# A retention mixer in three stages: batches in order at the start, and a weight conversion with three VectorE steps

## The chip, the cores and the metric

The kernel runs on one core of a Trainium2 chip. Times are device microseconds (us) of one execution, from start to end on that core. The inputs lie in the chip's memory at the start, and the output must lie there at the end.

## The reference

Three layers follow each other. The first is retention over 8 batches of 576 rows with 8 heads of 64, the second a token mixer of low rank followed by a two-layer network with 512, 2048 and 512 columns, the third a channel mixer on each row and the row before it. Cut to what is computed:

```
# q, k, v: (8, 8, 576, 64) float32
scores = matmul(q, k.T) / sqrt(64)
ret    = scores * D           # D[h, i, j] = gamma[h] ** (i - j) for i >= j, else 0
x      = matmul(ret, v)       # float32, then (8, 576, 512)

h  = x.T @ U @ V              # U: (576, 32), V: (32, 576), float64
u  = x + h.T
x  = u + maximum(u @ w_ch1, 0) @ w_ch2     # (512, 2048) and (2048, 512), float64

xk = mu_k * x + (1 - mu_k) * x_prev        # x_prev: one row earlier, zero in row 0
xr = mu_r * x + (1 - mu_r) * x_prev
k  = maximum(xk @ w_k, 0)                  # (512, 1024), float64
v  = k * k @ w_v                           # (1024, 512), float64
out = sigmoid(xr @ w_r) * v                # (512, 512), float64
```

U, V and the five weight matrices arrive as float64, and the kernel makes float32 of them on the chip.

## The kernel before

The rows of all batches are 4608, in nine blocks of 512. Every dense product is computed in three passes on pairs of tiles, a rounded high part (names ending in `h`) and the rest (names ending in `l`): high by high, low weight by high, high weight by low.

*Stage one* covers retention, the token mixer and the first dense product. A batch is cut into nine chunks of 64 rows. In a chunk TensorE computes the scores (`scores`, line 358), the product of the queries with the state carried over from the earlier chunks (`inter`, line 383), the chunk's addition to the state (`own`, line 399) and its own output (line 411). VectorE multiplies the scores by the decay table (tile `pm`, line 370), scales the product with the state (`y`, line 432), adds to the state (`w`, line 444; in the first chunk a copy, line 442) and adds up the output, transposed, in `xt` (line 450; in the first chunk a copy, line 448). The scores and the decay of a chunk are issued one step ahead. After every second chunk four transposes bring 128 rows into their natural order (`natural`, line 458) and four small products add to x.T @ U (`low_rank`, line 479). Once a batch has all nine chunks, `low_rank_sum` collects this, eight small products and additions (`mix`, lines 508 and 512) make u in `xt`, and `mix_store` splits it into high and low parts (lines 191 and 192), stores it (lines 519 and 520) and puts sixteen dense tiles on the list `ready`. A dense tile (`hidden`, tile `h`) is twelve matmuls at line 204, then ReLU on ScalarE (line 210) and a store (line 211). From here on they fill TensorE between the chunks.

*Weights.* `convert` makes float32 of a 128x512 piece of float64, in stages that `slot` moves on by one: the load (line 157); `flush`, an absolute value on ScalarE (line 100); `fill`, four VectorE steps (lines 106, 107, 111 and 116) that take the high words, set what is too small to zero, shift and mask the exponent and put sign and fraction together; and `split`, where ScalarE rounds to the high part (line 124) and GpSimd subtracts (line 125). U comes first, then group 0 of w_ch1 (`w1_0`, four pieces), V (two pieces of 288 columns), and groups 1 to 3.

*What sets the order.* Up to line 744 the code's own order is the order on each engine (`manual_schedule`), and each engine works through its own list and waits where something isn't there. Transfers are issued by SyncE, in order as well. The list `seq` in lines 587 to 592 gives the chunks: four chunks of batch 0, then one of batch 1 and one of batch 0 in turn until batch 0 ends, then the rest of batch 1, then the other batches one after another. `step_of` issues one step of it: loads of q, k and v ahead (line 652), the chunk, a slot of conversion (line 671), mixes if no dense tile is ready, and up to two dense tiles (lines 675 and 678) with what is due between them (transposes, `low_rank`, mixes). With one mix after each of its three passes, a dense tile also takes mixes along, and moves the conversions on by one where there are none (line 550). In lines 522 and 523 the dense tiles that are ready when batch 1 ends are sorted, so that those of the first group of w_ch1 come first.

*Stage two* is the second dense product (`project`, lines 237, 238 and 241), for which the stored h is loaded again and split, with the conversions of w_ch2 (line 696) and of the third layer's weights w_k, w_r and w_v beside it. *Stage three* is the channel mixer: `key_chunk` (products at line 760, square at line 766), `gate_tile` (line 779) and `value_tile` (line 794). From line 746 on the framework's scheduler sets the order.

Of the kernel before, what the change touches and what calls it, by code (L numbers as in the profile page):

```python
# [9 lines left out]
F32 = mybir.dt.float32  # L10
F32R = mybir.dt.float32r
BF16 = mybir.dt.bfloat16
U32 = mybir.dt.uint32
# [26 lines left out]
def retention_mixer_kernel(ctx: ExitStack, tc: tile.TileContext, io):  # L40
# [43 lines left out]

    TINY = float(np.array(897 << 20, np.uint32).view(np.float32))


    def convert(fetch, parts, p, n, after=None, eng=nc.gpsimd):  # L90
        got = {}

        def load():
            got["raw"] = fetch()

        def flush():
            w = got["raw"].bitcast(U32).rearrange("p (n t) -> p n t", t=2)
            got["lo"], got["hi"] = w[:, :, 0], w[:, :, 1]
            got["a"] = cv.tile([128, 512], F32, tag="ca", name="ca", bufs=2)[:p, :n]
            nc.scalar.activation(got["a"], got["hi"].bitcast(F32), AF.Abs)  # L100

        def fill():
            h, l = parts()
            a, lo, hi = got["a"], got["lo"], got["hi"]
            f = got["f"] = cv.tile([128, 512], F32, tag="cf", name="cf", bufs=3)[:p, :n]
            nc.vector.scalar_tensor_tensor(f, a, TINY, hi.bitcast(F32), op0=ALU.is_ge, op1=ALU.mult)  # L106
            nc.vector.tensor_scalar(  # L107
                a.bitcast(U32), f.bitcast(U32), 3, 0x3FFFFFFF,
                op0=ALU.logical_shift_left, op1=ALU.bitwise_and,
            )  # L110
            nc.vector.scalar_tensor_tensor(  # L111
                f.bitcast(U32), f.bitcast(U32), 0xC0000000, a.bitcast(U32),
                op0=ALU.bitwise_and, op1=ALU.bitwise_or,
            )
            whole = f if l is not None else h
            nc.vector.scalar_tensor_tensor(  # L116
                whole.bitcast(U32), lo, 29, f.bitcast(U32),
                op0=ALU.logical_shift_right, op1=ALU.bitwise_or,
            )

        def split():
            h, l = parts()
            if l is not None:
                nc.scalar.copy(h, got["f"])
                eng.tensor_tensor(l, got["f"], h.bitcast(F32), op=ALU.subtract)

        return [load, flush, fill, split] + ([after] if after else [])

    waiting, going = [], []

# [168 lines left out]
    with ExitStack() as st:  # L299
# [120 lines left out]
        def by_pair(x):  # L420
            return x.rearrange("p (a r) i -> p a r i", r=2)

        def leave(i):
# [14 lines left out]
            if c < NL - 1:  # L438
                d = t[:, :, 128:256].rearrange("p r (a x) -> p a r x", x=D)
                new = a2.tile([128, NP, D], F32, tag="wst", name=f"w{b}_{c}", bufs=4)  # L440
                if c == 0:
                    nc.vector.tensor_copy(by_pair(new), d)
                else:
                    nc.vector.tensor_tensor(by_pair(new), d, by_pair(wst[b]), op=ALU.add)
                wst[b] = new
            own_x = t[:, :, 0:128].rearrange("p r (a i) -> p a r i", i=L)
            if c == 0:
                nc.vector.tensor_copy(x, own_x)
            else:
                nc.vector.tensor_tensor(x, own_x, by_pair(y), op=ALU.add)  # L450

# [62 lines left out]
        def mix_store(b):  # L514
            o = (b + 1) * BT - b * S
            u = xt.pop(b)
            split_u(b, BT - o, u[:, :, :o], o)
            split_u(b + 1, 0, u[:, :, o:], S - o)
            nc.sync.dma_start(u_blk[b][:, :, BT - o:], u[:, :, :o])
            nc.sync.dma_start(u_blk[b + 1][:, :, :S - o], u[:, :, o:])  # L520
            ready.extend((b, f) for f in range(NF))
            if b == 1:
                ready.sort(key=lambda x: (x[1] >= 4, x))
            if b == B - 1:
                ready.extend((b + 1, f) for f in range(NF))

# [55 lines left out]
                    lambda s=s: nc.scalar.copy(vst[64:96, s], low[64:96].bitcast(F32)), nc.vector,  # L582
                ))

        LEAD = 4
        seq = [(0, c) for c in range(LEAD)]
        for c in range(NL - LEAD):
            seq += [(1, c), (0, c + LEAD)]  # L590
        seq += [(1, c) for c in range(NL - LEAD, NL)]
        seq += [(b, c) for b in range(2, B) for c in range(NL)]
        N = len(seq)
        FIRST = 2 * NL
        units = []
        for i, (b, c) in enumerate(seq):
            if c % 2 == 0:
# [50 lines left out]

        def step_of(i):
            b, c = seq[i]  # L650
            first = i < FIRST
            load_to(i + (7 if first else 4))
            if i + 1 < N:
                nb, ncx = seq[i + 1]
                if ncx % 2 == 0:
                    scale_k(nb, ncx // 2)
            if i + 1 < N:
                scores(i + 1)
            inter(i)
            if i + 1 < N:  # L660
# [1 line left out]
            own(i)  # L662
            leave(i)
            if c % 2 == 1 or c == NL - 1:
                wait = 4 if i < 8 else 2
                plan(i + 1, natural, b, c // 2)
                plan(i + wait, low_rank, b, c // 2)
                if c == NL - 1:
                    plan(i + wait, low_rank_sum, b)
                    plan(i + wait + 1, later, b)  # L670
            if first and (i < 10 or i % 2 == 0):
                slot()
            if not ready:
                mixes(4)
            hidden(1)
            for fn, args in due.pop(i, []):
                fn(*args)
            hidden(1)

        for i in range(N):  # L680
            step_of(i)
# [203 lines left out]
```

## Time and profile before

| | us |
|---|---|
| median of 3 runs | 1497.29 (1496.33 to 1497.86) |
| the profiled execution | 1495.31 |
| its span, first to last instruction | 1493.40 |
| TensorE busy | 1443.6 (97% of the span) |
| TensorE weight loads, beside its matmuls | 1164.9 (78%) |
| VectorE busy | 611.7 (41%) |
| ScalarE busy | 491.2 (33%) |
| GpSimd busy | 239.0 (16%) |
| granted TensorE clock, mean | 0.98 of full speed |

The span is what the trace covers; the execution's own time is 1.91 us longer. A share of busy time is a mean over the stages, and the rows further down take the span apart. In the views, PE is TensorE, PEld its weight loads, DVE VectorE, ACT ScalarE, POOL GpSimd and SPq the issue of transfers by SyncE. A granted clock (PEclk) of 1.00 is 2.4 GHz and 0.50 is 1.2 GHz; what lies between is a mean over a stretch. A releaser is what ended a wait.

### The profile page before, as it was taken

The page shows a single profiled execution, that of the slowest core. Times are in us where ns is not written, and L with a number is a line of the kernel's source. Part 1 is how long each engine was busy: PE and PEld are TensorE (multiplying, and loading weights), DVE is VectorE, ACT ScalarE, POOL GpSimd, SP SyncE. Part 2 cuts the span into 40 slices and gives each one's busy share as a digit, 9 for nine tenths or more (in the row PEclk, how much of TensorE's full clock was granted, in tenths as well). Part 3 has the DMA queues.
Part 4 walks back from the last instruction along what each step waited for, and adds up shares of the span by engine and source line. Part 5 has one row for each costly group of instructions (what it writes and reads, how often), then busy time and mean ns, then how long its engine had stood idle before and what let it go on. Part 6 is the DMA issues. An engine that isn't in the chain of part 4 may idle for free. (4 is left out here: it accounts for less than half of the span.)

```text
span 1493.4 us, 25018 instructions
## 1 busy us (share of the span) xinstructions
PE 1443.6 (97%) x10524; PEld 1164.9 (78%) x10524; DVE 611.7 (41%) x1020; ACT 491.2 (33%) x839; POOL 239.0 (16%) x216
## 2 busy tenths in 40 slices
PE   5679999999999999999999999999999999999998
PEld 4557777777777778888888888777888888888887
DVE  5976323131322375693322222484342343243240
ACT  2333323222222343432111211244444443444341
POOL 3422001010010032130000000024201211211220
PEclk6789999999999999999999999999999999999999
DMA  9535455454433465774443355451110110110000
GB/s 331 222 104 202 150 171 170 144 171 162 169 130 122 158 213 187 255 239 158 138 146 113 125 169 169 136 168 57 48 57 15 43 57 22 36 57 22 8 29 29
DMA packets 76897, 190.41 MB, mean 127 GB/s; under 512 B 10672, under 2 KB 17072, under 8 KB 76784
## 3 DMA queue, kind: packets, MB, share of 16 engines
q1 hardware_dynamic: 76784, 188.80, 37.4%
q8 instruction: 83, 1.36, 0.4%
q14 instruction: 30, 0.25, 0.1%
HBM read 122.71 MB, written 66.06 MB: 126 GB/s over the span
## 5 line engine op out<-in xcount | busy, mean ns | idle before, releaser
L210 ACT ACTIVATE hs<-h 128x512 f32<-128x512 f32 x144 | 85.6, 595 | 308.4 <-PE h L204 276.8
L225 DVE TENSOR_TENSOR hl<-hr,hh 128x1024 fp32r<-128x1024 f32 x72 | 87.7, 1226 | 159.1 <-PE c L238 100.8
L224 ACT CAST hh<-hr 128x1024 fp32r<-128x1024 f32 x72 | 75.6, 1050 | 232.5 <-DVE hl L225 65.0
L768 POOL TENSOR_TENSOR kl<-ks,kh 128x512 fp32r<-128x512 f32 x72 | 94.1, 1308 | 354.6 <-ACT kh L767 353.1
L370 DVE TENSOR_TENSOR pm<-up,dtab 128x256 f32<-128x256 f32 x72 | 30.4, 423 | 206.6 <-PE up L383 171.5
L798 DVE TENSOR_TENSOR o<-v,g 128x512 f32<-128x512 f32 x36 | 24.9, 692 | 185.8 <-PE v L794 185.8
L766 DVE SCALAR_TENSOR_TENSOR ks<-k,ka 128x512 f32<-128x512 f32 x72 | 49.7, 690 | 117.5 <-ACT ka L764 68.4
L291 ACT CAST mh<-m 128x512 fp32r<-128x512 f32 x72 | 44.8, 623 | 115.4 <-DVE tp L284 82.7
L329 POOL TENSOR_TENSOR kv<-kv,ktab 128x512 f32<-128x512 f32 (+1 forms) x40 | 41.0, 1028 | 199.6 <-DMA kv<-in_kv 164.3
L767 ACT CAST kh<-ks 128x512 fp32r<-128x512 f32 x72 | 44.5, 620 | 56.7 <-DVE ks L766 56.7
L287 DVE SCALAR_TENSOR_TENSOR m<-x2l,mu,tp 128x512 f32<-128x512 f32 x72 | 53.7, 751 | 13.5 <-ACT tp L278 6.2
L358 PEld LDWEIGHTS up<-qk 64*64 64x64 f32 x1152 | 26.3, 145 | 41.8 <-issue 32.5
L255 POOL COPY edge<-x 128x1 f32<-128x1 f32 x36 | 14.4, 401 | 270.6 <-DVE x L254 270.6
L111 DVE SCALAR_TENSOR_TENSOR cf<-cf,ca 128x512 uint32<-128x512 uint32 (+3 forms) x56 | 56.8, 1014 | 1.9
L278 ACT ACTIVATE tp<-x2l,omu 128x511 f32<-128x511 f32 x72 | 51.5, 715 | 17.8 <-DMA x2l<-xb 17.8
L512 DVE TENSOR_TENSOR xt<-mx,xt 128x256 f32<-128x256 f32 (+1 forms) x64 | 28.8, 457 | 68.8 <-PE mx L508 68.7
L237 PE MATMUL c<-hh,w_1h 128*128 128x512 f32 x144 | 56.3, 391 | 0.6 <-ACT hh L224 0.6
L764 ACT ACTIVATE ka<-k 128x512 f32<-128x512 f32 x72 | 42.8, 598 | 40.5 <-PE k L760 39.5
L238 PE MATMUL c<-hh,w_1l 128*128 128x512 f32 x144 | 56.1, 390 | 0.0
L794 PE MATMUL v<-wv_0h,kl 128*128 128x512 f32 x144 | 56.1, 390 | 0.0
L238 PE MATMUL c<-hh,w_3l 128*128 128x512 f32 x144 | 56.1, 390 | 0.0
L238 PE MATMUL c<-hh,w_0l 128*128 128x512 f32 x144 | 56.1, 390 | 0.0
(155 smaller groups left out, 3424.1 us busy)
## 6 DMA issues: line engine op xcount, KB each, us to landing
hb<-hs SPq DMA_DIRECT2D x144, 256.0 KB, 2.3
hr<-hb SPq DMA_DIRECT2D x72, 512.0 KB, 5.0
qk<-in_qk SPq DMA_DIRECT2D x32, 512.0 KB, 4.7
kv<-in_kv SPq DMA_DIRECT2D x32, 512.0 KB, 5.5
w_raw<-in_moe_w_ch SPq DMA_DIRECT2D x32, 512.0 KB, 4.7
ur<-ub SPq DMA_DIRECT2D x18, 512.0 KB, 4.4
xb<-x SPq DMA_DIRECT2D x36, 256.0 KB, 3.2
x2l<-xb SPq DMA_DIRECT2D x18, 512.0 KB, 4.3
```

The costliest lines, as they stand in the source:

```text
L111: nc.vector.scalar_tensor_tensor(f.bitcast(U32), f.bitcast(U32), 0xC0000000, a.bitcast(U32), op0=ALU.bitwise_and, op1=ALU.bitwise_or,)
L210: nc.scalar.activation(h, hps.pop((t, f)), AF.Relu)
L224: nc.scalar.copy(h, r)
L225: nc.vector.tensor_tensor(l, r, h.bitcast(F32), op=ALU.subtract)
L237: nc.tensor.matmul(acc[t][o], w.part(0, f % 4, oo), hh, start=(f == 0), stop=False)
L238: nc.tensor.matmul(acc[t][o], w.part(1, f % 4, oo), hh, start=False, stop=False)
L278: nc.scalar.activation(tp[:, 1:], xk[:, :BT - 1], AF.Copy, scale=omu[:, j, k:k + 1])
L287: nc.vector.scalar_tensor_tensor(m, xk, mu[:, j, k:k + 1], tp, op0=ALU.mult, op1=ALU.add)
L291: nc.scalar.copy(hk, m)
L766: nc.vector.scalar_tensor_tensor(sq, ps, 0.0, a, op0=ALU.max, op1=ALU.mult)
L768: nc.gpsimd.tensor_tensor(kl, sq, kh.bitcast(F32), op=ALU.subtract)
L794: nc.tensor.matmul(ps, x[:, f % 2, io_], wv[f // 4].part(lo, f % 4), start=(j == 0), stop=(j == len(ops) - 1))
```

## The change

Six things are different.

1. The list of chunks is simply batch after batch. Loads of q, k and v run five chunks ahead throughout, before it was seven in the first two batches and four after.
2. In the first two batches every step has a conversion slot. Mixes without a dense tile beside them come all nine at once, and only from batch 1 on.
3. A step of the first two batches issues one dense tile. From batch 2 on it is two, except in chunks 4 and 7, where it is one.
4. The list of ready dense tiles is no longer sorted when batch 1 ends.
5. The first ScalarE step of a conversion is a copy scaled by 2^-112 in place of the absolute value. What is too small becomes zero or is shifted out by this scaling, and the VectorE step at line 106 is gone; the other three take their sign and exponent from the scaled copy.
6. In the first chunk of each batch the two copies, of the state and of the output, are made by ScalarE.

```diff
-    TINY = float(np.array(897 << 20, np.uint32).view(np.float32))
+    DOWN = 2.0 ** -112
...
-        def flush():
+        def down():
...
-            nc.scalar.activation(got["a"], got["hi"].bitcast(F32), AF.Abs)
+            nc.scalar.activation(got["a"], w[:, :, 1].bitcast(F32), AF.Copy, scale=DOWN)
...
-            nc.vector.scalar_tensor_tensor(f, a, TINY, hi.bitcast(F32), op0=ALU.is_ge, op1=ALU.mult)
             nc.vector.tensor_scalar(
-                a.bitcast(U32), f.bitcast(U32), 3, 0x3FFFFFFF,
+                f.bitcast(U32), a.bitcast(U32), 3, 0x7FFFFFFF,
                 op0=ALU.logical_shift_left, op1=ALU.bitwise_and,
             )
             nc.vector.scalar_tensor_tensor(
-                f.bitcast(U32), f.bitcast(U32), 0xC0000000, a.bitcast(U32),
+                f.bitcast(U32), a.bitcast(U32), 0x80000000, f.bitcast(U32),
                 op0=ALU.bitwise_and, op1=ALU.bitwise_or,
             )
...
                 if c == 0:
-                    nc.vector.tensor_copy(by_pair(new), d)
+                    nc.scalar.copy(by_pair(new), d)
...
             if c == 0:
-                nc.vector.tensor_copy(x, own_x)
+                nc.scalar.copy(x, own_x)
...
             ready.extend((b, f) for f in range(NF))
-            if b == 1:
-                ready.sort(key=lambda x: (x[1] >= 4, x))
...
-        LEAD = 4
-        seq = [(0, c) for c in range(LEAD)]
-        for c in range(NL - LEAD):
-            seq += [(1, c), (0, c + LEAD)]
-        seq += [(1, c) for c in range(NL - LEAD, NL)]
-        seq += [(b, c) for b in range(2, B) for c in range(NL)]
+        seq = [(b, c) for b in range(B) for c in range(NL)]
...
-            first = i < FIRST
-            load_to(i + (7 if first else 4))
+            load_to(i + 5)
...
-                wait = 4 if i < 8 else 2
+                wait = 4 if i < 6 else 2
...
-            if first and (i < 10 or i % 2 == 0):
+            if b < 2:
                 slot()
             if not ready:
-                mixes(4)
+                mixes(9 if b else 0)
             hidden(1)
             for fn, args in due.pop(i, []):
                 fn(*args)
-            hidden(1)
+            if b > 1 and c not in (4, 7):
+                hidden(1)
```

Where this moves instructions is shown at three places. The first is VectorE's list in the start, around the conversion of the third piece of `w1_0` before. In the names, `pm7` is the decay of chunk 7 of the list (counted from 0), `y5` the scaled product of chunk 5, `w0_4` the state of batch 0 after its chunk 4, `xt0` the output of batch 0, and `raw2` the third piece.

```order
L432 TENSOR_TENSOR y5_479<-up6_443,qtab_109 128x256
L444 TENSOR_TENSOR w0_4_481<-dn5_462,w0_3_374 128x256
L450 TENSOR_TENSOR xt0_213<-dn5_462,y5_479 128x4x64
L106 SCALAR_TENSOR_TENSOR cf_488<-ca_428,w1_0_raw2_386 128x512
L107 TENSOR_SCALAR ca_428<-cf_488 128x512
L111 SCALAR_TENSOR_TENSOR cf_488<-cf_488,ca_428 128x512
L116 SCALAR_TENSOR_TENSOR cf_488<-w1_0_raw2_386,cf_488 128x512
L370 TENSOR_TENSOR pm7_525<-up7_508,dtab_108 128x256
L432 TENSOR_TENSOR y6_544<-up7_508,qtab_109 128x256
L444 TENSOR_TENSOR w1_1_546<-dn6_527,w1_0_418 128x256
```

In the same place of the changed kernel, with the conversion of the second piece:

```order
L432 TENSOR_TENSOR y4_421<-up5_385,qtab_109 128x256
L444 TENSOR_TENSOR w0_4_423<-dn4_404,w0_3_368 128x256
L450 TENSOR_TENSOR xt0_209<-dn4_404,y4_421 128x4x64
L107 TENSOR_SCALAR cf_428<-ca_377 128x512
L111 SCALAR_TENSOR_TENSOR cf_428<-ca_377,cf_428 128x512
L116 SCALAR_TENSOR_TENSOR cf_428<-w1_0_raw1_316,cf_428 128x512
L370 TENSOR_TENSOR pm6_461<-up6_444,dtab_108 128x256
L432 TENSOR_TENSOR y5_480<-up6_444,qtab_109 128x256
L444 TENSOR_TENSOR w0_5_482<-dn5_463,w0_4_423 128x256
```

A conversion is three rows instead of four, and the following chunk's rows belong to the same batch: before, `w0_4` is followed by `w1_1`, the state of batch 1, now by `w0_5`.

The second place is TensorE's list where the dense work begins, before, with `mx0` the mixes of batch 0, `xn` the transposes, `gall` the low-rank products, `up` and `dn` the products of chunks and `h0_0` the first dense tile.

```order
L411 MATMUL dn18_1218<-pm18_1174,kv2_0_808 64x64 x8
L508 MATMUL mx0_0_1_1239<-vst_114,gt0_1078 128x320
L508 MATMUL mx0_1_1_1242<-vst_114,gt0_1078 128x320
L508 MATMUL mx0_2_1_1245<-vst_114,gt0_1078 128x320
L508 MATMUL mx0_3_1_1248<-vst_114,gt0_1078 128x320
L479 MATMUL gall_499<-xs1_3_1205,ust_113 32x128 x4
L458 MATMUL xn1_4_1255<-ident_112,xt1_417 64x128 x4
L358 MATMUL up20_1263<-qk2_1_929 64x64 x8
L383 MATMUL up20_1263<-qk2_0_806,w2_0_1236 64x64 x8
L399 MATMUL dn19_1282<-kv2_0_808 64x64 x8
L411 MATMUL dn19_1282<-pm19_1216,kv2_0_808 64x64 x8
L204 MATMUL h0_0_1322<-uh0_0_1304,w1_0h0_377 128x512 x2
L204 MATMUL h0_0_1322<-uh0_1_1305,w1_0h2_486 128x512 x2
```

And in the changed kernel:

```order
L358 MATMUL up13_872<-qk1_2_624 64x64 x8
L383 MATMUL up13_872<-qk1_1_504,w1_2_845 64x64 x8
L399 MATMUL dn12_891<-kv1_1_506 64x64 x8
L411 MATMUL dn12_891<-pm12_824,kv1_1_506 64x64 x8
L508 MATMUL mx0_0_0_923<-vst_114,gt0_799 128x256
L508 MATMUL mx0_1_0_926<-vst_114,gt0_799 128x256
L508 MATMUL mx0_2_0_929<-vst_114,gt0_799 128x256
L508 MATMUL mx0_3_0_932<-vst_114,gt0_799 128x256
L508 MATMUL mx0_0_1_935<-vst_114,gt0_799 128x320
L508 MATMUL mx0_1_1_938<-vst_114,gt0_799 128x320
L508 MATMUL mx0_2_1_941<-vst_114,gt0_799 128x320
L508 MATMUL mx0_3_1_944<-vst_114,gt0_799 128x320
L204 MATMUL h0_0_965<-uh0_0_947,w1_0h0_371 128x512 x2
```

The dense tiles began behind chunk 19 of the list, and the eight mixes stood in two groups of four behind two chunks; now they begin behind chunk 12, and the eight mixes stand together ahead of them.

The third place is TensorE's list in stage three, behind the order written out by hand: `k0_2` and `k0_3` are key tiles of the first block, `r0_0` and `r0_1` gate tiles. Before:

```order
L760 MATMUL k0_2_9452<-mh0_0_1_9026,wk_0l2_6904 128x512 x2
L760 MATMUL k0_2_9452<-ml0_0_0_9027,wk_0h0_6819 128x512 x2
L760 MATMUL k0_2_9452<-ml0_0_1_9028,wk_0h2_6903 128x512 x2
L779 MATMUL r0_0_9570<-wrh0_7179,mh0_1_0_9147 128x512 x2
L779 MATMUL r0_0_9570<-wrh2_7263,mh0_1_1_9148 128x512 x2
L779 MATMUL r0_0_9570<-wrl0_7180,mh0_1_0_9147 128x512 x2
L779 MATMUL r0_0_9570<-wrl2_7264,mh0_1_1_9148 128x512 x2
L779 MATMUL r0_0_9570<-wrh0_7179,ml0_1_0_9149 128x512 x2
L779 MATMUL r0_0_9570<-wrh2_7263,ml0_1_1_9150 128x512 x2
L779 MATMUL r0_1_9585<-wrh0_7179,mh0_1_0_9147 128x512 x2
L760 MATMUL k0_3_9471<-mh0_0_0_9025,wk_0h0_6819 128x512 x2
```

And in the changed kernel:

```order
L750 MATMUL k0_2_9396<-ml0_0_0_8979,wk_0h0_6783 128x512 x2
L750 MATMUL k0_2_9396<-ml0_0_1_8980,wk_0h2_6865 128x512 x2
L750 MATMUL k0_3_9415<-mh0_0_0_8977,wk_0h0_6783 128x512 x2
L750 MATMUL k0_3_9415<-mh0_0_1_8978,wk_0h2_6865 128x512 x2
L750 MATMUL k0_3_9415<-mh0_0_0_8977,wk_0l0_6784 128x512 x2
L750 MATMUL k0_3_9415<-mh0_0_1_8978,wk_0l2_6866 128x512 x2
L750 MATMUL k0_3_9415<-ml0_0_0_8979,wk_0h0_6783 128x512 x2
L750 MATMUL k0_3_9415<-ml0_0_1_8980,wk_0h2_6865 128x512 x2
```

The framework's scheduler had put the gate tile `r0_0` and two products of `r0_1` between the third and the fourth key tile; now the key tiles follow each other, and `r0_0` stands behind `k0_7`. The diff doesn't touch this code.

## Rows read from the trace of the kernel before

**Rows 1.** Busy time, granted clock, share and rate of transfers, by stretches.

```profile
core 0: us, PE busy (x) PEld busy (x) DVE busy (x) ACT busy (x) POOL busy (x), PEclk, DMA share, GB/s
...
20.00:40.00 20.00, 9.18 (x216) 7.34 (x216) 16.78 (x29) 5.98 (x11) 5.28 (x4) 0.57 0.96 336
...
60.00:80.00 20.00, 11.83 (x342) 8.96 (x340) 17.93 (x36) 6.31 (x13) 7.11 (x7) 0.84 0.01 2
...
120.00:500.00 380.00, 380.00 (x4571) 295.31 (x4570) 111.60 (x261) 104.99 (x196) 40.12 (x38) 1.00 0.45 155
500.00:560.00 60.00, 57.38 (x247) 45.29 (x246) 40.23 (x56) 26.02 (x45) 14.42 (x10) 1.00 0.65 213
...
950.00:1030.00 80.00, 73.63 (x305) 58.69 (x304) 54.60 (x73) 36.32 (x57) 24.08 (x20) 0.96 0.46 150
```

**Rows 2.** VectorE's groups, 20 to 85 us, with mean duration and releasers.

```profile
line engine op names shapes xcount | busy us, mean ns | idle before us <-releasers
L106 DVE SCALAR_TENSOR_TENSOR cf<-ca,w_raw 128x512 f32<-128x512 f32 x9 | 8.8, 976 | 4.0 <-ACT ca L100 4.0
L111 DVE SCALAR_TENSOR_TENSOR cf<-cf,ca 128x512 uint32<-128x512 uint32 x9 | 7.2, 805 | 0.3
L107 DVE TENSOR_SCALAR ca<-cf 128x512 uint32<-128x512 uint32 x9 | 7.0, 774 | 0.3
L370 DVE TENSOR_TENSOR pm<-up,dtab 128x256 f32<-128x256 f32 x15 | 6.3, 419 | 2.8 <-PE up L358 1.9 <-PE up L383 0.9
L116 DVE SCALAR_TENSOR_TENSOR cf<-w_raw,cf 128x512 uint32<-128x512 uint32 x9 | 6.2, 692 | 0.3
```

**Rows 3.** Timeline, 21 to 124 us: start, duration, instruction, wait before it.

```profile
21.88 0.66 ACT L100 ACTIVATE ca<-w_raw 128x512 f32<-128x512 f32 x1 [13.78 <-DMA w_raw<-in_moe_w_ch]
...
22.57 0.69 DVE L106 SCALAR_TENSOR_TENSOR cf<-ca,w_raw 128x512 f32<-128x512 f32 x1 [3.77 <-ACT ca L100]
...
29.89 0.42 DVE L370 TENSOR_TENSOR pm<-up,dtab 128x256 f32<-128x256 f32 x1
...
30.23 0.41 DVE L432 TENSOR_TENSOR y<-up,qtab 128x256 f32<-128x256 f32 x1
...
30.79 0.71 PE L358 MATMUL up<-qk 64*64 64x64 f32 x16 [2.64 <-DVE y L432]
...
32.09 0.68 PE L411 MATMUL dn<-pm,kv 64*64 64x64 f32 x16
...
82.72 1.68 DVE L512 TENSOR_TENSOR xt<-mx,xt 128x320 f32<-128x320 f32 x4
...
86.30 0.73 PE L204 MATMUL h<-uh,w_0h 128*128 128x512 f32 x2 [0.52 <-ACT uh L191]
...
94.89 0.35 SPq L157 DMA_DIRECT2D w_raw<-in_moe_w_ch  x1
...
98.63 0.67 ACT L100 ACTIVATE ca<-w_raw 128x512 f32<-128x512 f32 x1 [0.30 <-DMA w_raw<-in_moe_w_ch]
...
114.19 0.46 PE L358 MATMUL up<-qk 64*64 64x64 f32 x16
...
119.03 0.60 PE L458 MATMUL xn<-ident,xt 128*128 128x128 f32 x4
...
119.39 1.18 PE L204 MATMUL h<-uh,w_0h 128*128 128x512 f32 x4
...
122.33 0.46 PE L358 MATMUL up<-qk 64*64 64x64 f32 x16
...
123.42 1.19 PE L204 MATMUL h<-uh,w_0h 128*128 128x512 f32 x4
```

**Rows 4.** VectorE's first conversion step on the value weights, 940 to 1030 us.

```profile
L106 DVE SCALAR_TENSOR_TENSOR cf<-ca,wv_raw 128x512 f32<-128x512 f32 x8 | 7.7, 958 | 0.0
```

**Rows 5.** Timeline around 1000 us.

```profile
1000.07 2.48 DVE L254 TENSOR_TENSOR x<-c,ur 128x512 f32<-128x512 f32 x4
...
1003.80 1.64 PE L760 MATMUL k<-mh,wk_0h 128*128 128x512 f32 x4 [2.26 <-DVE ks L766]
...
1017.02 1.27 PE L760 MATMUL k<-mh,wk_1h 128*128 128x512 f32 x4 [3.12 <-DVE ks L766]
```

More of the change, by code (lines that the diff above doesn't have):

```diff
@@ L94, in load @@
             got["raw"] = fetch()
-        def flush():
+        def down():
             w = got["raw"].bitcast(U32).rearrange("p (n t) -> p n t", t=2)
-            got["lo"], got["hi"] = w[:, :, 0], w[:, :, 1]
+            got["lo"] = w[:, :, 0]
             got["a"] = cv.tile([128, 512], F32, tag="ca", name="ca", bufs=2)[:p, :n]
-            nc.scalar.activation(got["a"], got["hi"].bitcast(F32), AF.Abs)
+            nc.scalar.activation(got["a"], w[:, :, 1].bitcast(F32), AF.Copy, scale=DOWN)
         def fill():
             h, l = parts()
-            a, lo, hi = got["a"], got["lo"], got["hi"]
+            a, lo = got["a"], got["lo"]
             f = got["f"] = cv.tile([128, 512], F32, tag="cf", name="cf", bufs=3)[:p, :n]
-            nc.vector.scalar_tensor_tensor(f, a, TINY, hi.bitcast(F32), op0=ALU.is_ge, op1=ALU.mult)
             nc.vector.tensor_scalar(
-                a.bitcast(U32), f.bitcast(U32), 3, 0x3FFFFFFF,
+                f.bitcast(U32), a.bitcast(U32), 3, 0x7FFFFFFF,
                 op0=ALU.logical_shift_left, op1=ALU.bitwise_and,
@@ L125, in split @@
                 eng.tensor_tensor(l, got["f"], h.bitcast(F32), op=ALU.subtract)
-        return [load, flush, fill, split] + ([after] if after else [])
+        return [load, down, fill, split] + ([after] if after else [])
     waiting, going = [], []
@@ L583, in prep_v @@
                 ))
-        LEAD = 4
-        seq = [(0, c) for c in range(LEAD)]
-        for c in range(NL - LEAD):
-            seq += [(1, c), (0, c + LEAD)]
-        seq += [(1, c) for c in range(NL - LEAD, NL)]
-        seq += [(b, c) for b in range(2, B) for c in range(NL)]
+        seq = [(b, c) for b in range(B) for c in range(NL)]
         N = len(seq)
-        FIRST = 2 * NL
+        FIRST = NL
         units = []
@@ L656, in step_of @@
                     scale_k(nb, ncx // 2)
-            if i + 1 < N:
                 scores(i + 1)
```

## The prediction

> **What bounds the kernel now.** I read the busy times by stage first [rows 1]. TensorE is busy for all of 120 to 500 us at full clock, and nearly all of the rest, so work can't be shortened there; only what it stands idle or runs at half clock can be won. That is in three places. Up to 120 us it is part busy: 9.18 of 20 us in 20 to 40 at a granted clock of 0.57 (0.5 is the lower level, 1.2 GHz; it had mostly been waiting before), 11.83 of 20 in 60 to 80. Around 500 to 560 us 2.6 us are missing, and in 950 to 1030 us 6.4 us, at a clock of 0.96.
>
> The second view is VectorE's groups in 20 to 85 us [rows 2], since VectorE is the engine that is busy there (16.78 and 17.93 of 20). A weight conversion is four VectorE steps with means of 976, 774, 805 and 692 ns, 3.25 us together. The third is the timeline of that stretch [rows 3]: the first conversion of a 128x512 weight starts at 22.57, held by ScalarE, which waited 13.78 us for the raw weight; the last mix addition of batch 0 ends at 82.72 + 1.68 = 84.40; the first dense product of h starts at 86.30. From there TensorE has filler. So the time from 22.57 to 84.40, 61.8 us, is VectorE working through conversions, chunk steps and mixes in its order, and the end of it opens the dense work. The last views are VectorE's conversions and the timeline around 1000 us [rows 4, 5]: TensorE waits 2.26 us at 1003.80 and 3.12 us at 1017.02 for VectorE's squares, which stand behind the conversion of the value weights.
>
> **The change part by part.** *The start on VectorE.* Counted in the order between the first weight conversion and the last mix addition of batch 0, nine weight conversions become eight, and the chunk instructions (decay, leave and state) between them go from 56 to 32, since half of the second batch no longer stands there. A removed first step is 0.69 us when nothing is in its way [rows 3], 0.72 with the gap behind it, and 0.98 in the mean [rows 2]. I take 0.72: what lengthens the steps is GpSimd work beside them, as the spread between 0.69 and 0.98 on the same shape suggests, and no GpSimd instruction goes away. So eight first steps are 5.8 us; the ninth conversion, now behind the point, 3.25; 24 chunk instructions at 0.34 from start to start (29.89 to 30.23 [rows 3]) are 8.2; two first steps on V, with 288 columns, an estimated 1.0. From 61.8 that leaves 43.5 us. The stretch also starts sooner: four pairs of q, k and v tiles instead of five are queued ahead of the first raw weight, 1.05 MB less at 336 GB/s [rows 1], 3.1 us, so about 19.5. The mixes then end at 63; waits of 2.8 us before the decay [rows 2] belonged to the crossing of two batches, and with half of them gone I take 62, with 57 and 69 as ends (all of 0.98 and all waits gone; or none of this and the raw weights late).
>
> The Trainium skill (SBUF — State Buffer, section "SBUF: two separate sides") has a rule against a larger gain here: VectorE in a two-port mode or with two inputs in SBUF and GpSimd share a port pair, which one of them holds for a whole instruction. By that rule the blocked time moves to the steps that stay. The trace agrees, with 0.69 us alone and 0.98 in the mean for one shape [rows 2, 3]; by the rule the eight steps give 5.8 us, and without it 7.8.
>
> *From the mixes to steady work.* Dense tiles now stand one in each chunk of batch 1 from its fourth chunk on, with two conversions a chunk. VectorE has to pass, from 62: the low halves of u, 4 us (as from 84.40 on, estimated from the gap to the first dense product and four such steps); then seven conversions at 3.25 - 0.72 = 2.53, 17.7; four chunks' steps at 4 x 0.34, 5.4. At 62 + 27 = 89 the sixth dense tile is free; before it TensorE has the rest of a chunk, 1.0, and itself 2.94 (119.39 to 122.33 [rows 3]): 93. In the kernel before, the sixth dense tile was finished at 114.19, but four more chunks, three transposes, three low-rank groups and eight mixes were done too: 4 x 1.09 (122.33 to 123.42 [rows 3]) + 3 x 0.6 + 3 x 0.3 + 8 x 0.2 (the last two estimated from the columns of a chunk and a dense tile) = 8.7 us. So 93 compares with 105.5: **12.5 us**, with 5 and 20 as ends. From there both kernels are TensorE at full clock with the same work, and the order holds no chunk without a dense tile; sixteen tiles come and go with each batch.
>
> The two copies of each batch's first chunk go from VectorE to ScalarE. VectorE's is taken as 0.42, like the decay of the same 256 columns [rows 3]; on ScalarE I bound it by that 0.42 and the 0.66 of its 512-column step, and price it at nothing: the first pair stands before ScalarE has work, the others beside dense tiles. The scaling on ScalarE takes the place of one of the same size (0.66 [rows 3]): nothing, within 0.1 us each.
>
> *Weights of the second product.* In the end of the retention stage two mixes no longer stand alone, and the conversion of w2 starts three dense tiles sooner: of the 2.6 us missing in 500 to 560 I take **1**, ends 0 and 2.6.
>
> *Value weights.* 950 to 1030 lacks 6.4 us, and 0.04 of 80 us in clock, 3.2: 9.6 us to win at most. Eight removed steps are 7.7 us with and 5.8 without what blocked them [rows 4]. Five stand ahead of the additions at 1000.07 [rows 5]; since VectorE also waited before, I move these by 3.3, and with them the wait that ended at 1003.80, to 1000.5. But the order now has fourteen gate products behind the key tiles, which used to fill that time: 14 x 0.245 (2.94 / 12) = 3.4 us. So the first wait gives nothing. To the second wait it was 13.2 us, with two removed steps in it, 1.4 to 2.5: now about 1011.8, which stands for 1013.6 before. That is 1.8, and with half of the clock's loss 1.6: **3 us**, ends 0 and 9.
>
> *The sum* is 12.5 + 1 + 3 = 16.5, and 1 more for the waits of the second batch's mixes, which now stand between dense tiles: 17.5. The profiled execution took 1495.31 (span 1493.40), which gives 1477.8; the median of the runs shown is 1.98 higher, so **1479.5**. With the ends taken together by halves rather than all on one side, 1467 to 1490.
>
> **Rivals.** *Weights late behind stores.* The raw weights of groups 3 and 4 now stand in SyncE's queue behind batch 0's store and then behind each dense tile's. A raw tile landed 3.7 us after its issue (94.89 to 98.63 [rows 3]). The first of them is issued at about 62 + 5.7 and is ready for VectorE 10.1 us after the mixes; its turn is at 4 + 2.53 + 1.36 + 2.53 = 10.4. If it is later than that, VectorE, whose order is fixed, holds the chunk behind it too. One landing lost in each of three chunks takes 11 of the 12.5 us: 1490. For it speaks the thin margin, against it that the transfers rested in 60 to 80 us (share 0.01, 2 GB/s [rows 1]), so there is room.
>
> *Lead without effect.* VectorE's work is only moved: if its order is held by something else up to the mixes (transfers, at a share of 0.96 in 20 to 40), only the removed steps count, 5.8 + 1.0, and the two later places, 4: 1487.
>
> *Slower: the chain of one batch.* Two batches used to alternate, so that a chunk's state was ready a step ahead. Alone, each chunk goes products, decay, state, products. At half clock a chunk's products took from 30.79 to 32.77 (32.09 + 0.68), 2.0 us [rows 3], and in every second one a transpose, 0.60 at full clock (119.03 [rows 3]), is there twice as long. They hide behind a conversion of 2.53 as long as they fit; where they don't fit at all, a step is 2.0 + 0.6 + 1.4 + 2.5 + 0.5 for hand-overs, 7.0 instead of 3.9. Nine steps of it cost 28 us, 15.4 more than the gain; with the 4 that the later places give, 11.4 slower: 1509. Against it: scores may start a step's 0.68 us before its last VectorE instruction, and VectorE waited only 2.8 us for products in 20 to 85 [rows 2].
>
> By the Trainium skill (TensorE: Matmul & The Clock Gate, section "HAM oscillation — how this bites in real kernels") gaps put the array back on its low clock. The trace agrees, with 0.57 in 20 to 40 us; this rule makes the last rival's condition likelier and changes no other term.
>
> **Chances.** The forecast 0.70, late weights 0.11, lead without effect 0.11, slower 0.08. The range is 1467 to 1491: it holds the forecast's own spread and the two rivals that still gain. What a measurement of this kernel can tell from no change is about 0.2%, 3 us. Faster: 0.70 + 0.11 + most of the late weights, 0.90; within: 0.03; slower: the last rival, less where it decides only in part, 0.07.
>
> **What would show it.** The last mix addition of batch 0 ending near 62 us and the first dense product 2 us later; the sixth dense tile done near 93; TensorE full from about 95. The step means of a conversion: three steps at about 2.5 us in sum shows the blocking moved, 1.9 that it went. Around 1000 us a wait of key products for squares shorter than 3 us, and no gate product ahead of the fourth key tile. The forecast is wrong if the mixes end after 70, if VectorE waits for raw weights between the mixes and 93, or if TensorE has new idle time after 120.

## The result, and the profile after

| | before | after |
|---|---|---|
| median, us | 1497.57 (1496.33 to 1499.49, 4 runs) | 1480.74 (1479.86 to 1484.15, 4 runs) |
| ratio | | 0.9891 (0.9871 to 0.9910) |
| the profiled execution; its span | 1495.31; 1493.40 | 1484.15; 1482.0 |
| mean granted clock | 0.980 | 0.984 |
| VectorE, ScalarE, GpSimd busy | 611.7, 491.2, 239.0 | 565.5, 496.6, 235.1 |

The change takes 16.8 us off; 1479.5 was forecast, a gain of 17.8 on the median of 1497.29 known then. The profiled execution of after is the longest of its four, 3.4 us above the median; a second profile of the same kernel (its span 1479.7) stands with the experiments. The stretches of [rows 1], after:

```profile
core 0: us, PE busy (x) PEld busy (x) DVE busy (x) ACT busy (x) POOL busy (x), PEclk, DMA share, GB/s
20.00:40.00 20.00, 13.20 (x282) 10.42 (x284) 19.40 (x35) 7.89 (x16) 9.32 (x8) 0.50 1.02 359
...
60.00:80.00 20.00, 16.10 (x250) 12.17 (x249) 15.87 (x27) 9.05 (x16) 6.78 (x5) 0.84 0.68 245
80.00:100.00 20.00, 17.31 (x232) 13.53 (x225) 14.92 (x25) 8.19 (x16) 9.84 (x9) 0.94 0.59 212
...
120.00:500.00 380.00, 377.64 (x4645) 294.68 (x4637) 109.16 (x264) 105.64 (x202) 32.02 (x32) 1.00 0.46 157
500.00:560.00 60.00, 57.70 (x247) 46.91 (x246) 31.14 (x36) 26.29 (x45) 16.50 (x12) 0.97 0.56 192
...
950.00:1030.00 80.00, 76.79 (x328) 62.42 (x329) 49.39 (x72) 39.97 (x65) 23.08 (x20) 0.98 0.37 121
```

Two things are to be seen beside the fuller 60 to 80. In 120 to 500 us TensorE never stood idle before; now 2.36 us are missing. And 950 to 1030 us lacks 3.2 us where it lacked 6.4. The VectorE groups of the start, 20 to 62 us, answer to [rows 2]:

```profile
L111 DVE SCALAR_TENSOR_TENSOR cf<-ca,cf 128x512 uint32<-128x512 uint32 x8 | 7.3, 908 | 0.3
L107 DVE TENSOR_SCALAR cf<-ca 128x512 uint32<-128x512 uint32 x8 | 7.0, 877 | 1.6 <-ACT ca L101 1.6
L116 DVE SCALAR_TENSOR_TENSOR cf<-w_raw,cf 128x512 uint32<-128x512 uint32 x8 | 5.5, 692 | 0.3
```

The three steps take 2.48 us together where four took 3.25. That is not 0.98 less, the mean of the removed one, but 0.77. The timeline of after answers to [rows 3, 5]; the columns are start, duration, instruction and the wait before it:

```profile
57.82 3.19 DVE L512 TENSOR_TENSOR xt<-mx,xt 128x256 f32<-128x256 f32 x8
...
61.37 2.17 PE L204 MATMUL h<-uh,w_0h 128*128 128x512 f32 x4 [0.89 <-ACT uh L191]
...
77.77 0.43 DVE L107 TENSOR_SCALAR cf<-ca 128x512 uint32<-128x512 uint32 x1 [1.05 <-ACT ca L101]
...
93.68 1.09 PE L204 MATMUL h<-ul,w_1h 128*128 128x512 f32 x4
...
132.32 0.46 PE L358 MATMUL up<-qk 64*64 64x64 f32 x16 [0.54 <-PE xn L458]
...
991.16 2.47 DVE L254 TENSOR_TENSOR x<-c,ur 128x512 f32<-128x512 f32 x4
...
994.62 1.19 PE L750 MATMUL k<-mh,wk_0h 128*128 128x512 f32 x4 [0.30 <-DVE ks L756]
...
1004.67 1.19 PE L750 MATMUL k<-mh,wk_1h 128*128 128x512 f32 x4 [1.59 <-DVE ks L756]
```

The last products of the sixth dense tile in the trace of before:

```profile
113.18 1.08 PE L204 MATMUL h<-ul,w_1h 128*128 128x512 f32 x4
```

The mixes of batch 0 end at 57.82 + 3.19 = 61.01 (before 84.40), the dense work starts at 61.37 (before 86.30), and the sixth dense tile is done at 93.68 + 1.09 = 94.77 (before 113.18 + 1.08 = 114.26). The row at 132.32 is new and comes once in each batch; the profile names TensorE's own transposes as its releaser, and what it really waits for is asked by second_tile_in_chunk_4. The two waits of key products are 0.30 and 1.59 instead of 2.26 and 3.12.

### The profile page after: what moved, and what is told of

The parts are those of the page before. It is cut to its first block, busy times and chain, and to the rows that moved or that the text cites. A ratio compares the mean times of both kernels' runs of the same rounds, so it can differ in the third digit from the quotient of the medians.

```text
span 1482.0 us, 25030 instructions
## 1 busy us (share of the span) xinstructions
PE 1439.7 (97%) x10524; PEld 1165.2 (79%) x10524; DVE 565.5 (38%) x948; ACT 496.6 (34%) x855; POOL 235.1 (16%) x216
## 4 chain that ended last, share of the span: by engine, by line
PE 90%; DMA 4%; DVE 4%; issue 1%; ACT 1%; SPq 0%; POOL 0%; DVEq 0%; ACTq 0%
PE h L204 26%; PE v L784 13%; PE k L750 12%; PE c L237 8%; PE c L238 8%; PE c L241 8%; PE r L769 7%; DMA w_raw<-in_moe_w_ch 2%; PE up L358 1%; PE xn L458 1%; DVE cf L111 1%; PE dn L411 1%; PE dn L399 1%; PE gall L479 1%; PE up L383 1%
## 5 line engine op out<-in xcount | busy, mean ns | idle before, releaser
L237 PE MATMUL c<-hh,w_0h 128*128 128x512 f32 x144 | 56.0, 389 | 0.0
L237 PE MATMUL c<-hh,w_2h 128*128 128x512 f32 x144 | 56.0, 389 | 0.0
L238 PE MATMUL c<-hh,w_2l 128*128 128x512 f32 x144 | 56.0, 389 | 0.0
L237 PE MATMUL c<-hh,w_3h 128*128 128x512 f32 x144 | 56.0, 389 | 0.0
```

The costliest lines, as they stand in the source:

```text
L237: nc.tensor.matmul(acc[t][o], w.part(0, f % 4, oo), hh, start=(f == 0), stop=False)
L238: nc.tensor.matmul(acc[t][o], w.part(1, f % 4, oo), hh, start=False, stop=False)
```

## The experiments

Each kernel ran beside the kernel before on the same chip; the ratio is to that kernel. The first table has every run, the second cuts the traces in two at places that all kernels have: the first product of the second layer (stage one ends there) and the last value product.

| run | median, us | ratio (95%) |
|---|---|---|
| again | 1481.48 | 0.9890 (0.9875 to 0.9905) |
| three_steps_only | 1478.16 | 0.9874 (0.9861 to 0.9888) |
| sequence_only | 1500.29 | 1.0018 (1.0009 to 1.0026) |
| value_weights_four | 1486.46 | 0.9928 (0.9916 to 0.9940) |
| one_slot | 1473.20 | 0.9841 (0.9827 to 0.9856) |
| two_tiles | 1517.63 | 1.0139 (1.0124 to 1.0155) |
| raw_earlier | 1480.60 | 0.9894 (0.9878 to 0.9911) |
| copies_on_vector | 1482.08 | 0.9899 (0.9885 to 0.9914) |
| four_steps_one_slot | 1488.23 | 0.9945 (0.9930 to 0.9960) |
| mixes_first | 1468.43 | 0.9811 (0.9796 to 0.9826) |
| mixes_first_raw_earlier | 1465.60 | 0.9794 (0.9778 to 0.9811) |
| second_tile_in_chunk_4 | 1462.68 | 0.9769 (0.9753 to 0.9786) |

| trace | mixes of batch 0 end | stage one ends | from there to the start of the last value product |
|---|---|---|---|
| before | 84.40 | 596.96 | 892.34 |
| after; again | 61.01; 61.39 | 589.87; 588.93 | 887.99; 886.59 |
| three_steps_only | 77.72 | 586.05 | 886.59 |
| sequence_only | 67.21 | 600.75 | 893.76 |
| value_weights_four | 61.13 | 587.21 | 892.27 |
| one_slot | 60.40 | 578.83 | 887.24 |
| raw_earlier | 59.39 | 582.60 | 891.30 |
| four_steps_one_slot | 67.08 | 588.93 | 894.35 |

**again**, the changed kernel unchanged.

> The changed kernel once more, unchanged. The profiled execution of it took 1484.15 us, the other three 1479.86 to 1481.26. Theory one: the difference is a loss of that one execution, the wait of 1.80 us near 512 us and the clock of 0.92 behind it; then a second profile has a span of 1477 to 1480 us and no wait over 0.6 us there, with the clock at 1.00. Theory two: this loss is in every execution; then the wait is there again and the span is near 1482.

Measured: the same median and a span of 1479.7. Near 503 and 515 us TensorE waits 1.02 and 0.33 us for ReLU, where the first profile had 0.50 and 1.80 and a clock of 0.92 behind it. A second place came out of the comparison, a key product that stands among the last projections, first in after and then in again:

```profile
950.72 0.96 PE L750 MATMUL k<-mh,wk_0h 128*128 128x512 f32 x3 [1.65 <-ACT mh L291]
```

```profile
948.37 0.98 PE L750 MATMUL k<-mh,wk_0h 128*128 128x512 f32 x3 [0.24 <-ACT mh L291]
```

It waits, through ScalarE and VectorE, for a transfer (x, loaded again), for 1.4 us longer in after, and the clock of 950 to 960 us is 0.83 there and 1.00 in again. So both theories hold in part: the waits are in every execution, their size varies with transfers, and a long one also costs clock. Up to 500 us after is 1.0 us ahead of again. The first place then costs it 1.9 us, the second 1.4 and the lower clock behind it as much again, and the first wait of key products is 1.4 shorter in it: 2.3 us between the two spans.

**three_steps_only** and **sequence_only** split the change in two: the kernel before with the new conversion alone (item 5), and the changed kernel with the old one (items 1 to 4 and 6). The edit is the conversion's hunk of the diff, put in or taken out.

> The kernel before with only the new conversion. Theory one, the parts add: about 6 us at the value weights (between the last projection and the end the traces show 6.2 us less) and about 6 us in the start, with the last mix addition of batch 0 near 78 instead of 84.4: 1485 us. Rival, the start is held by something other than VectorE's steps (the crossing of two batches, transfers): the mixes end at 83 or later and only the value weights gain: 1491 us.

> The changed kernel with the old conversion of four VectorE steps. Theory one: the last mix addition at 61 + 8 x 0.72 = 67 us, the value weights as before: 1480.7 + 6 + 6 = 1492.5 us, a gain of 5 on before. Rival, the sequence carries the start alone: mixes at 63 or earlier, 1487 us. The two kernels of this pair then add up to the whole gain of 16.8 us if the parts are independent; if they sum to clearly less, the parts need each other.

Measured: the conversion alone gives 19.7 us, more than the whole change. The sequence alone costs 2.4 us where 5 were expected to be gained. Both came out beyond either theory, on opposite sides; together they are 17.3 us, near the 16.4 of again, so the parts add up. Yet the mixes did what was expected, 77.72 and 67.21:

```profile
76.02 1.70 DVE L511 TENSOR_TENSOR xt<-mx,xt 128x320 f32<-128x320 f32 x4
```

```profile
64.02 3.19 DVE L513 TENSOR_TENSOR xt<-mx,xt 128x256 f32<-128x256 f32 x8
```

The first row is three_steps_only's last mix addition, the second are sequence_only's eight. In sequence_only the mixes end 17.2 us earlier than before and stage one ends 3.8 us later. So the time at which the dense work starts does not by itself set the end of stage one. In three_steps_only the sixth dense tile is done at 105.05 us, 9.2 us earlier than before, and stage one ends 10.9 earlier. What happens behind it is in sequence_only's next stretch, busy times as in [rows 1]:

```profile
80.00:100.00 20.00, 13.27 (x182) 9.96 (x180) 19.48 (x28) 7.68 (x14) 9.43 (x7) 0.91 0.63 231
```

VectorE is busy for 19.48 of 20 us and TensorE for 13.27: the conversions of groups 2 and 3 are still to come, two with each chunk. By 104.7 us all sixteen are made; in the trace of before only twelve are made by 103, and the other four between 122 and 135, beside full dense work. What the new order takes out of VectorE's start, chunks of the second batch, it fills with conversions.

**value_weights_four** takes the third place of the order by itself:

```diff
-                waiting.append(convert(fetch, parts, 128, 512))
+                waiting.append((convert4 if self.nm.startswith("wv") else convert)(fetch, parts, 128, 512))
```

> The changed kernel, with the old conversion of four steps for the value weights alone; by its order the gate tile r0_0 then stands ahead of the fourth key tile again. Theory one: the value weights are worth the 6.2 us between the two traces: 1487 us, with waits of key products for squares of about 2 and 3 us at the fourth and seventh key tile. Rival, they are worth the 3 us of the forecast and the rest belongs to the profiled execution: 1484 us.

Measured: 5.0 us slower than again, and the stretch behind stage one is 892.27, that of before, against 886.59. Both waits are back, the first with its size of before:

```profile
994.02 1.20 PE L792 MATMUL k<-mh,wk_0h 128*128 128x512 f32 x4 [2.26 <-DVE ks L798]
...
1007.19 2.08 PE L792 MATMUL k<-mh,wk_1h 128*128 128x512 f32 x4 [4.71 <-DVE ks L798]
```

The removed step of eight value conversions, with the order that the scheduler then makes, is worth 5.7 us in the traces, not 3.

**one_slot** asks whether VectorE's two conversions a chunk are the bound:

```diff
-            if b < 2:
+            if b < 2 and not ready:
                 slot()
```

> The changed kernel, in which a step has a slot of its own only as long as no dense tile is ready; behind the mixes of batch 0 one conversion comes with each chunk and dense tile instead of two. Theory one: from 61 to 93 us VectorE works through two conversions a chunk, and this is what the new order costs; with one, a chunk is 1.36 + 2.5 = 3.9 us of VectorE beside 4.0 to 4.6 of TensorE, so that TensorE sets the pace from 65 us on: 6 us less than the changed kernel, 1475.5, the sixth dense tile done near 88. Rival: dense tiles wait for raw weights or for converted weights of groups 2 and 3, which now come later: no gain, or up to 3 us slower than 1481.5.

Measured: 8.3 us less than the changed kernel, where 6 were expected. The dense work starts at the same time as there (60.77), but TensorE is nearly full from then on, and the sixth dense tile is done at 87.68 us, as expected. In one_slot's trace:

```profile
60.00:80.00 20.00, 19.23 (x305) 14.89 (x309) 15.11 (x29) 8.73 (x16) 5.15 (x4) 0.88 0.74 254
80.00:100.00 20.00, 20.00 (x290) 15.30 (x281) 13.07 (x24) 9.39 (x19) 9.60 (x8) 1.00 0.74 259
```

The same conversions are made by 97.0 us instead of 93.7 (after), and nothing waits for them.

**four_steps_one_slot** is sequence_only with that same edit.

> The changed kernel with the old conversion of four steps and, as in the run one_slot, one conversion for each chunk behind the mixes of batch 0. It asks what the new order of chunks is worth when VectorE isn't loaded with two conversions a chunk. Theory one: the sequence alone lost (1500.3) because sixteen conversions stand ahead of steady work, twelve before; with one a chunk, VectorE needs 1.36 + 3.25 = 4.6 us beside 4.0 to 4.6 of TensorE, the sixth dense tile is done near 95 instead of 105: 1490 to 1492 us, faster than before. Rival: the new order costs by itself (transfers, waits at each batch): 1497 or more.

Measured: 12.1 us less than sequence_only and 0.9945 of before. The new sequence (items 1 to 4) is worth 8.3 us as soon as the conversions behind the mixes come one a chunk; how much of that is the order of the chunks alone, no run separates.

**two_tiles** takes out the exception for chunks 4 and 7:

```diff
-            if b > 1 and c not in (4, 7):
+            if b > 1:
                 hidden(1)
```

> The changed kernel with two dense tiles in every chunk from batch 2 on, chunks 4 and 7 too. Theory one: the wait of TensorE for scores that comes once in each batch in the trace (0.50, 0.43, 0.29, 0.18, 0.38, 0.53 us, with the low halves of u on VectorE beside one dense tile) goes: 2.3 us less, 1479. Rival: these waits cost what is shown but the tiles then run out in chunk 8, and TensorE waits there instead: 1481.5 or more.

Measured: 36 us slower, on the rival's side (1481.5 or more), but by far more than waits of this size. With two in each of nine chunks 18 tiles go in a batch in which 16 come. The stock is used up after a few batches, and then the mixes, which otherwise stand between the passes of a dense tile, stand alone. Here are two of them and their stretch, in two_tiles:

```profile
464.55 0.39 PE L508 MATMUL mx<-vst,gt 96*128 96x256 f32 x1 [0.52 <-DVE xt L512]
465.45 0.38 PE L508 MATMUL mx<-vst,gt 96*128 96x256 f32 x1 [0.52 <-DVE xt L512]
```

```profile
460.00:475.00 15.00, 10.79 (x137) 7.30 (x129) 9.07 (x20) 3.72 (x7) 2.60 (x3) 0.77 0.39 133
```

4.2 of 15 us idle at a mean clock of 0.77; such rows of eight mixes stand near 255, 325, 395, 465 and 530 us. The kernel before had two tiles a chunk too, but its dense work began in the third batch with the tiles of two batches coming one after the other. In the new order the exception is what keeps sixteen going for sixteen coming.

**raw_earlier** and **copies_on_vector** each change one small thing, raw_earlier in the first piece of the diff, copies_on_vector in the other two:

```diff
-        return [load, down, fill, split] + ([after] if after else [])
+        return [load, lambda: None, down, fill, split] + ([after] if after else [])
...
-                    nc.scalar.copy(by_pair(new), d)
+                    nc.vector.tensor_copy(by_pair(new), d)
...
-                nc.scalar.copy(x, own_x)
+                nc.vector.tensor_copy(x, own_x)
```

> The changed kernel with one empty stage between the load of a raw weight and its ScalarE step. Theory one: in 60 to 80 us ScalarE waits 3.2 and 3.6 us for raw weights, VectorE 1.0 and 1.0 behind it and TensorE 3.0 for a copy queued behind it on ScalarE; these go, and the waits for ReLU near 503 and 512 us too: 3 us less, 1478.5. Rival: the start is VectorE's conversions anyway, and each comes one slot later: 1481.5 to 1484.

> The changed kernel with the two copies of each batch's first chunk on VectorE as before. Theory one, the forecast: worth nothing, 1481.5 within 1. Rival: the copies on ScalarE stand behind conversions that wait for raw weights, and cost: 1480 or less.

Measured: the copies are worth nothing on either engine (1482.1 against 1481.5), as forecast. raw_earlier is the same in its total too, but for another reason than its rival: stage one ends 6.3 us earlier than in again, and 4.7 are given back behind it, at the value weights, whose conversions also come one slot later and now stand ahead of a square there. In raw_earlier:

```profile
996.38 1.54 PE L750 MATMUL k<-mh,wk_1h 128*128 128x512 f32 x4 [3.99 <-DVE ks L756]
```

Not all of the 6.3 us is late raw weights. The empty stage also leaves seven conversions ahead of the mixes instead of eight, and they end 2.0 us earlier than in again. From there to the end of the sixth dense tile (91.28) it takes 31.9 us, where again takes 35.8 and after 33.8; so late raw weights cost the changed kernel some 2 to 4 us there. Where, the waits of after in 60 to 100 us show (engine, line, what it waited for, total us, times, longest):

```profile
ACT ca L101 <- DMA w_raw<-in_moe_w_ch: 9.2, 5, 3.6
...
PE gall L479 <- ACT xs L468: 4.4, 2, 3.0
```

ScalarE waits for a raw weight, and behind it on ScalarE stands the copy of a transpose that TensorE needs for its low-rank products.

**mixes_first**, **mixes_first_raw_earlier** and **second_tile_in_chunk_4** build on one_slot, one edit on the other, in this order (the first two pieces of the diff, the next two, the last):

```diff
-                    plan(i + wait + 1, later, b)
+                    plan(i + wait + (b > 0), later, b)
...
+            if b and not ready:
+                mixes(9)
             if b < 2 and not ready:
                 slot()
-            if not ready:
-                mixes(9 if b else 0)
...
-        return [load, down, fill, split] + ([after] if after else [])
+        return [load, *rest, down, fill, split] + ([after] if after else [])
...
-                waiting.append(convert(fetch, parts, 128, 512))
+                waiting.append(convert(fetch, parts, 128, 512, rest=[lambda: None] * (self.nm[:2] in ("w1", "w2"))))
...
-            if b > 1 and c not in (4, 7):
+            if b > 1 and c not in (6, 7):
```

> The kernel of the run one_slot, with the mixes of batch 0 one chunk earlier and ahead of that step's conversion. Theory one: TensorE stood with its first mix products from 51.96 to 58.29 us while VectorE made two conversions and a chunk's steps; without them the mixes end near 54 instead of 60.4 and the dense work starts 6 us sooner, of which TensorE's chunk and its waits take a part: 1468 to 1470 us. Rival: the eight low-rank copies on ScalarE and GpSimd's subtraction end only near 51, or the tiles wait for weights: 1472 to 1474.

> The kernel of the run mixes_first with the empty stage behind the load for the weights of the first and second product alone. Theory one: the waits of ReLU behind ScalarE's waits for raw weights near 494 and 503 us (1.4 us in one_slot) go, and the value weights keep their places: 1 to 2 us less than mixes_first. Rival: same as mixes_first within 0.5, since conversions come a slot later in the start.

> The kernel of the run mixes_first_raw_earlier, with the chunks of one dense tile from batch 2 on being 6 and 7 instead of 4 and 7. It asks what the wait for scores is that TensorE has once in each batch (0.53, 0.43, 0.32, 0.22, 0.34, 0.50 us in that run, sum 2.3). Theory one: in chunk 4 a single dense tile, 2.9 us with a transpose, stands beside the low halves of u, 2.76 us on VectorE, ahead of the steps that free the scores' place; with a second tile there the waits go: 1463.3 us. Rival: a chunk with one tile has this wait wherever it stands: 1465.6 again.

Measured: 4.8, 2.8 and 2.9 us less, step by step, where about 4, 1 to 2 and 2.3 were expected. In the second the waits for ReLU (1.7 us in mixes_first) are gone, and the mixes end 1.0 us earlier as well. The mixes end at 54.07 in mixes_first, with six conversions ahead of them instead of eight, and TensorE is busy for all of 60 to 120 us. In the last one the wait that came once in each batch is gone, though chunks 6 and 7 now have one dense tile each; its 120 to 500 us show no idle TensorE. So the wait belonged to chunk 4, where the low halves of u stand on VectorE. It runs in 1462.68 us, 0.9769 of the kernel before, and beats the changed kernel by 18 us.

## Why the prediction was right, and where its terms were off

*The time and its range* hold, but terms were off in opposite directions, and the parts of the change don't share the gain as the text suggests. Of the three signs by which the prediction would know itself wrong, the first did not come (the mixes ended at 61, not after 70); the other two did, in small size: VectorE waited for raw weights between the mixes and 93 us, and TensorE had new idle time after 120 us.

*The mixes*: forecast 62, measured 61.01. One piece was tried alone: the removed steps ahead of the mixes were put at 5.8 us and 1.0 for V, and sequence_only ends them 5.8 us later than again and 6.2 later than after.

*The blocking moves to the steps that stay.* Forecast were about 2.5 us for three steps if so, 1.9 if not; measured 2.48, 2.41 in again and 2.47 in three_steps_only up to its mixes (20 to 78 us). sequence_only, the same order as after with four steps, has 3.33. Which step takes the longer time varies: the one that needs 0.43 us where nothing is in its way has means of 877, 812 and 685 ns in these three. The trace of after shows what goes with it. Of the 48 steps of 128x512 conversions between 20 and 95 us, fifteen took 0.98 us or more, and each of these began while a GpSimd instruction ran; of the other 33 only one did. One such pair:

```profile
81.35 1.47 POOL L125 TENSOR_TENSOR w_2l<-cf,w_2h 128x512 fp32r<-128x512 f32 x1 [1.29 <-ACT w_2h L124]
...
81.71 1.66 DVE L116 SCALAR_TENSOR_TENSOR cf<-w_raw,cf 128x512 uint32<-128x512 uint32 x1
```

GpSimd ends at 82.82 us, and the step, 0.69 us long when alone, 0.55 us after that. By the Trainium skill (SBUF — State Buffer, section "SBUF: two separate sides") one of the two engines holds a shared port pair for a whole instruction and the other is blocked. The trace agrees, though no run takes the GpSimd work away.

*From the mixes to steady work*: forecast were 93 for the sixth dense tile and 12.5 us. Measured are 94.77 and, in again, 97.21, so 10.7 and 8.3 us by the same reckoning. The stretch from the mixes to this tile took 33.8 and 35.8 us, 31 were forecast. The gap is largely the rival with late weights, to which 0.11 was given, at some 2 to 4 us instead of 11. It did not cost VectorE a landing in each chunk, as it was put: VectorE waited twice behind ScalarE (1.03 and 1.05 us in after, 1.72 and 0.97 in again), and TensorE waited through ScalarE's order. In raw_earlier, without these waits, the stretch took 31.9.

*"From there both kernels are TensorE at full clock with the same work"* failed in a small way: 2.36 us in 120 to 500 us, the six waits for scores. The low halves of u (2.77 us on VectorE at 128.79 us) stood beside a single dense tile in chunk 4; second_tile_in_chunk_4 takes the waits away.

*The second product's weights*: forecast 1. Of the 2.6 us that were missing in [rows 1], 2.3 are missing in after and 1.5 in again; 0.3 to 1.1.

*The value weights* were mis-sized: forecast 3, within 0 to 9; measured 4.4 (after) and 5.75 (again, three_steps_only), and 5.7 by value_weights_four. "The first wait gives nothing" was wrong, 2.26 became 1.70 in again and 1.69 in three_steps_only (the 0.30 of after stands behind its long wait at 950.72, by which TensorE comes later); the second lost half, and the four products behind the waits take 1.19 to 1.21 us, not 1.64 and 1.27 [rows 5], so that in again, with a clock of 1.00 in 950 to 1030, all of the clock's loss there went where half was counted.

*The waits of the second batch's mixes* were counted twice. In the trace of before they stand ahead of the end of the sixth dense tile, so that the 12.5 us already hold the 1 us that was added for them:

```profile
99.91 0.36 PE L508 MATMUL mx<-vst,gt 96*128 96x256 f32 x1 [1.35 <-ACT xs L468]
...
103.25 0.58 PE L508 MATMUL mx<-vst,gt 96*128 96x256 f32 x1 [2.08 <-DVE xt L512]
```

*The number is in part luck.* Term by term the traces give 10.7 - 2.4 + 0.3 + 4.4 = 13.0 us for after and 8.3 - 2.3 + 1.1 + 5.75 = 12.9 for again, where 17.5 were added up (the sum as written comes to 1479.8, not 1479.5). The medians lie 16.8 us apart, and no run shows where the other 4 us are.

*What the sum hid.* The 12.5 us of the start were written as one gain of fewer steps and of chunks that no longer stand ahead. Fifteen removed first steps at 0.72 (eight ahead of the mixes, seven behind) and 1.0 for V are 11.8 of it. So by the prediction's own rule the order of chunks gives next to nothing: with 3.25 us a conversion the sixth tile would come 11.8 us later than 93, near 105, where 105.5 stood for before. sequence_only has it at 105.07. The step that failed is that the text never asked what either part does alone. The rival "lead without effect" (0.11) had half of this: VectorE's work is only moved and the removed steps count. But its condition, that something else holds the mixes, did not come true, and its 1487 was too high because it counted the eight removed steps ahead of the mixes and not the seven behind, and the value weights at 3. *The slower rival*, the chain of one batch, had the right sign for the sequence and the wrong mechanism: VectorE was busy for 19.48 of 20 us there and not waiting for products.

What stays open: by their profiled executions the two kernels differ by 11.2 and, with again, 13.6 us, by their medians by 16.8. Executions of one kernel scatter by up to 4.3 us here, and a single trace can't tell where all of that lies.

## What to carry to other kernels

An earlier start of the main work is worth only as much as the engine that feeds it has less to do until that work is steady: count its instructions up to there, not up to the start. When a change has two parts, price each alone by the same rule; here one carried more than the whole and the other lost 2.4 us. And a rate at which a stock is used must be weighed against the rate at which it fills: two tiles in 18 places against sixteen coming cost 36 us.

## What was not expected of the hardware

Leaving out one of four VectorE steps made the other three longer in sum: 2.48 us in the start instead of 2.27 before, and instead of 2.16 in sequence_only, which has the same order with four steps. So a step with a mean of 0.98 us (1.17 in sequence_only) was worth 0.77 (0.85). A raw weight that came late on ScalarE held TensorE for 3.0 us at 78.19 us of after, although the products that stood waiting needed nothing of that weight. And of waits of TensorE alike in size some were followed by a lower clock and some not: in after, 1.80 us near 512 us (0.92 in 500 to 515) and 1.65 us near 950 with 0.60 more behind it (0.83 in 950 to 960) were, and 1.70 us near 992 us in again (1.00 in 980 to 1000) was not.
